# One kernel, a new order: a table of places for dynamic convolution, layer norm and feed-forward

## The chip, the cores and the metric

One NeuronCore of a Trainium2 chip runs the whole program. The metric is the device time of one execution in microseconds (us), the median of several. Five engines work side by side, each through its own list of instructions in its own fixed order: TensorE (PE; its weight loads are shown apart as PEld), VectorE (DVE), ScalarE (ACT), GpSimd (POOL) and SyncE (SP, which only issues transfers). They meet through semaphores. Transfers are carried by 16 DMA engines, whoever issues them.

## The reference

```python
# x (8, 4224, 192), weight_gen (8, 4224, 8 heads, 7 taps)
w = softmax(weight_gen, axis=-1)                 # over the 7 taps of each head
x_unf = the token and its 6 predecessors, zeros ahead of each sequence
out = np.einsum('bshk,bskhg->bshg', w, x_unf)    # 24 channels to a head
...
x = out                                          # (8, 4224, 192)
xn = (x - mean) / sqrt(var + 1e-06) * g_ln
return x + np.maximum(xn @ w_ch1, 0.0) @ w_ch2   # 192 -> 768 -> 192
```

`g_ln`, `w_ch1` and `w_ch2` come as 64-bit floats; everything else is 32-bit.

## The kernel before

The 33,792 tokens lie as 128 partitions by 264 columns: partition p holds 264 tokens that follow each other, and a column is 128 tokens, one on each partition. The work is cut three ways.

- **Chunks** (mostly 6 columns, 47 of them) are the unit of the convolution. SP loads x into a ring of 36 columns (`load`, L425). DVE makes the seven products of x and tap weights in four instructions, `c0` to `c3` (L507; three of them make two products at once, into two halves of a buffer `pr`, the fourth makes one, into `y`). POOL then issues two transfers that add one half of a `pr` to the other inside the DMA engines (`d0`, `d1`, L513; called adds below), and adds four halves to `y` with instructions of its own (`a0` to `a3`, L510). The first three chunks are small and are summed on PE (L532).
- **Parts** (mostly 12 columns, 25 of them) are the unit of the softmax weights and of the layer norm. ACT sums and squares each column (`sums` L571, `squares` L576), a few tiny instructions make the scale (`rstd` on ACT, `newton` on DVE, L603 to L608), ACT applies it (`xh`, L620) and makes a 16-bit copy (`hi`, L640), POOL makes the 16-bit remainder (`lo`, L642), and SP issues a transpose by DMA (`turn`, L646) into `xT`. The softmax of a load of 12 columns is `wload` (SP, L431), `max` and `sum` (DVE), `sub` and `less` (POOL, L451 and L458), `exp` and `log` (ACT).
- **Groups** (4 columns, 66 of them, numbered from 0; table entries are given by the group in which they begin) are the unit of the feed-forward part. A group has one `lo` and one `turn`. PE makes three `unit`s of 36 matmuls each from `xT` (L664), which go to two PSUM buffers `ph`; ACT writes relu as 16-bit numbers (`relu`, L679), and DVE their remainder (`hlo`, L681), which frees `ph`. The second product of a group runs one group later: `p0` and `p1`, 72 matmuls each (L715), between the next group's units. DVE adds the result to `y` (`f`, L767), and SP writes a chunk out (`u`, L775). For the last group, PE makes the second product in another form (L744).

At the start, SP also loads the two weight matrices; DVE, ACT, POOL and PE turn them into scaled 16-bit halves (names that begin with `w_`), and SP swaps halves of the first (`w_m`, L922), which has to land before the first `unit`.

**What sets the order.** The code records every operation with `op(engine, cost, (name, t), function, reads, writes)`, and the operation takes the next number from the table `PLACE[name]`. `Plan.order` sorts all operations by that number and issues them so; an engine's instructions stand in its list in this order and never overtake each other. The costs handed to `op` are not used for the order. The numbers run through all engines together. Which of a pool's buffers an operation gets also follows from the places:

```python
o.key, o.place = want, PLACE[want[0]][i]
...
out = sorted(self.ops, key=lambda o: o.place)
...
b.slot = min(range(len(tenant[b.pool])), key=lambda i: freed(tenant[b.pool][i]))
...
if o.kind in last:
    o.behind, last[o.kind] = last["turn" if o.kind == "add" else "add"], o
```

The last two lines keep adds and transposes apart: each add (`d0`, `d1`) waits until the last transpose placed ahead of it has landed, and each transpose until the last add placed ahead of it has. Nothing else orders transfers against each other.

The data the program needs between engines sets the other waits: a `turn` waits for `hi` and `lo`, the first `unit` of a group for its `turn`, and a third use of `ph` for an `hlo`.

## Time and profile before

| | |
|---|---|
| median of 3 runs | 884.35 us (879.41 to 884.49) |
| the profiled execution | 884.04 us |
| its span, first to last instruction | 882.2 us |
| PE busy | 822.3 us, 93% of the span |
| DVE, POOL, ACT busy | 740.9, 704.4, 690.1 us |
| mean granted clock of TensorE | 0.976 of full |

The profiled execution lies within 0.4 us of the median, and 1.84 us of it lie outside the span. A busy PE is one with a matmul in flight; a matmul that runs slowly is busy for longer, so the count of matmuls in a stretch tells more of progress than the busy time.

### The profile page before, as it was taken

What the parts mean: (1) busy time and instruction counts of PE and PEld (TensorE: products, weight loads), DVE (VectorE), ACT (ScalarE), POOL (GpSimd) and SP (SyncE); (2) the same over time, 40 slices, a digit from 0 to 9 for tenths busy, and PEclk for the clock granted to TensorE, in tenths of its full rate; (3) what the DMA queues carried; (4) which work ended last, traced back from release to release, by engine and by line L of the source; (5) the groups of instructions that cost most, each with busy time, mean ns of one, the idle gap of its engine ahead of it and who ended that gap; (6) DMA issues with size and microseconds to landing.
All of it is one profiled execution on the core that took longest, in us unless ns stands there. A gap on an engine that the chain in (4) does not pass through costs nothing.

```text
span 882.2 us, 37253 instructions
## 1 busy us (share of the span) xinstructions
PE 822.3 (93%) x16663; PEld 796.0 (90%) x16663; DVE 740.9 (84%) x670; ACT 690.1 (78%) x1796; POOL 704.4 (80%) x391
## 2 busy tenths in 40 slices
PE   5457899999999999999999999999999999989997
PEld 5237899999999899999999999999999999979997
DVE  7999999988999899899979889989998887844433
ACT  3689898998788769968897987978888887867421
POOL 4999999997989888799979889979998988735100
PEclk9759999999999999999999999999999999989999
DMA  8689687879996967777889798676878967553432
GB/s 222 150 194 197 142 182 187 182 153 214 214 199 134 215 140 156 168 150 154 171 170 202 146 218 181 165 168 161 199 126 172 213 134 136 110 83 51 108 74 82
DMA packets 135294, 141.66 MB, mean 161 GB/s; under 512 B 107238, under 2 KB 109166, under 8 KB 135134
## 3 DMA queue, kind: packets, MB, share of 16 engines
q1 hardware_dynamic: 122158, 88.94, 45.0%
q0 software_dynamic: 12672, 50.34, 29.3%
q8 instruction: 130, 2.13, 1.0%
q14 instruction: 30, 0.25, 0.1%
q10 hardware_dynamic: 304, 0.00, 0.0%
HBM read 36.43 MB, written 25.95 MB: 71 GB/s over the span
## 4 chain that ended last, share of the span: by engine, by line
PE 46%; POOL 30%; issue 8%; DMA 7%; DVE 5%; ACT 4%; SPq 0%; POOLq 0%; DVEq 0%; ACTq 0%
PE ph L664 23%; PE po L715 22%; POOL y L510 20%; POOL hl L642 4%; DMA xT<-hl 3%; POOL pr L513 3%; DVE pr L507 3%; DMA pr<-pr 3%; POOL e L451 1%; POOL e L458 1%; DVE hlo L681 1%; ACT junk L571 1%; ACT junk L576 1%; PE ph L744 1%; DMA x<-in_x_dram 1%
## 5 line engine op out<-in xcount | busy, mean ns | idle before, releaser
L510 POOL TENSOR_TENSOR y<-y,pr 128x1152 f32<-128x1152 f32 (+1 forms) x176 | 474.2, 2707 | 27.1 <-DVE y L507 13.1
L664 PE MATMUL ph<-xT,c_w 64*128 64x256 f16 x7128 | 419.4, 271 | 22.4 <-DMA xT<-hl 13.0
L664 PEld LDWEIGHTS <-c_w 64*128 64x128 f16 x7128 | 379.7, 95 | 38.8 <-DMA xT<-hl 15.0
L715 PE MATMUL po<-c_w2h,hh 64*128 64x192 f16 x3120 | 387.7, 243 | 6.0 <-DVE y L767 2.9
L715 PE MATMUL po<-c_w2h,hlo 64*128 64x192 f16 x3120 | 387.8, 243 | 1.5 <-issue 1.5
L715 PE MATMUL po<-c_w2l,hh 64*128 64x192 f16 x3120 | 387.7, 243 | 1.2 <-issue 1.2
L507 DVE TENSOR_TENSOR pr<-x,wn 128x2304 f32<-128x2304 f32 (+2 forms) x139 | 333.8, 2412 | 5.0 <-POOL y L510 2.9
L681 DVE SCALAR_TENSOR_TENSOR hlo<-ph,hh 128x1024 f16<-128x1024 f32 x198 | 239.4, 1219 | 97.7 <-ACT hh L679 96.6
L715 PEld LDWEIGHTS <-hh 64*128 64x128 f16 x6240 | 304.1, 94 | 9.9 <-issue 8.1
L679 ACT ACTIVATE hh<-ph 128x1024 f16<-128x1024 f32 x198 | 199.5, 1013 | 99.6 <-PE ph L664 92.0
L715 PEld LDWEIGHTS <-hlo 64*128 64x128 f16 x3120 | 172.4, 94 | 2.0 <-issue 1.8
L642 POOL TENSOR_TENSOR hl<-xh,hl 128x768 f16<-128x768 f32 x66 | 114.5, 1754 | 32.5 <-ACT hl L640 29.7
L620 ACT ACTIVATE xh<-y,s 128x192 f32<-128x192 f32 x264 | 125.5, 535 | 13.1 <-DVE s L608 5.5
L576 ACT ACTIVATE junk<-y,s 128x192 f32<-128x192 f32 x264 | 119.6, 453 | 7.7 <-PE po L715 1.0
L513 POOL DMA_DIRECT2D pr<-pr x88 | 85.0, 1065 | 44.2 <-DMA xT<-hl 17.0
L571 ACT ACTIVATE junk<-y 128x192 f32<-128x192 f32 x264 | 94.9, 360 | 19.9 <-POOL y L510 11.3
L767 DVE SCALAR_TENSOR_TENSOR y<-po,c_fs,y 128x768 f32<-128x768 f32 (+1 forms) x86 | 68.4, 813 | 5.0 <-PE po L715 4.6
L507 DVE TENSOR_TENSOR y<-x,wn 128x1152 f32<-128x1152 f32 (+2 forms) x47 | 59.6, 1267 | 1.7 <-ACT wn L470 1.7
L640 ACT ACTIVATE hl<-xh 128x768 f16<-128x768 f32 x66 | 55.0, 837 | 3.3 <-DMA xT<-hl 1.4
L571 ACT ACTIVATION_READ_ACCUMULATOR junk<-y 128x1 f32 x264 | 49.5, 187 | 0.0
L576 ACT ACTIVATION_READ_ACCUMULATOR junk<-y,s 128x1 f32 x264 | 49.4, 187 | 0.0
L451 POOL TENSOR_TENSOR e<-w,mx 128x672 f32<-128x672 f32 (+2 forms) x23 | 33.8, 1470 | 7.8 <-DVE mx L449 6.6
(76 smaller groups left out, 285.2 us busy)
## 6 DMA issues: line engine op xcount, KB each, us to landing
pr<-pr POOLq DMA_DIRECT2D x80, 576.0 KB, 6.8
x<-in_x_dram SPq DMA_DIRECT2D x40, 576.0 KB, 6.2
out_dram<-y SPq DMA_DIRECT2D x40, 576.0 KB, 6.1
w<-in_weight_gen_dram SPq DMA_DIRECT2D x21, 336.0 KB, 5.0
pr<-pr POOLq DMA_DIRECT2D x8, 384.0 KB, 4.5
x<-in_x_dram SPq DMA_DIRECT2D x5, 384.0 KB, 5.6
out_dram<-y SPq DMA_DIRECT2D x4, 384.0 KB, 3.5
x<-in_moe_w_ch_dram SPq DMA_DIRECT2D x1, 1152.0 KB, 13.3
```

The costliest lines, as they stand in the source:

```text
L507: E.tensor_tensor(out=ov, in0=xv, in1=wv, op=ALU.mult)
L510: Q.tensor_tensor(out=flat(0), in0=flat(0), in1=flat(k), op=ALU.add)
L513: return Q.dma_start(flat(to), flat(k), accum_op=ALU.add, max_dma_last_dim=CHUNK * D * 4)
L571: A.activation(junk, at(y)[:, j, :], AF.Identity, scale=-SQ / D, accum_out=at(s4)[:, 3, t : t + 1])
L576: A.activation(junk, at(y)[:, j, :], AF.Square, scale=SQ, bias=at(s4)[:, 3, t : t + 1], accum_out=at(s4)[:, 0, t : t + 1])
L620: A.activation(paired(xh, t), at(y)[:, i, :].rearrange("p (c q) -> p c q", q=P // 2), AF.Identity, bias=at(s4)[:, 3, g + t : g + t + 1], s ...
L642: lambda xh=xh, hl=hl: Q.tensor_tensor(out=halves(hl, True), in0=pairs(xh), in1=halves(hl, False), op=ALU.subtract),
L664: T_.matmul(ph[:, r, v * 2 * P : (v + 1) * 2 * P], W["w1"][rows, WB[r][c], w, f : f + P], xv[rows, a, c, :, :], start=(v == 0 and k == 0), ...
L679: lambda: A.activation(at(hh)[:, us, :], at(ph), AF.Relu), [ph], [(hh, u)])
L681: lambda: V.scalar_tensor_tensor(out=at(hlo)[:, us, :], in0=at(ph), scalar=0.0, in1=at(hh)[:, us, :], op0=ALU.max, op1=ALU.subtract),
L715: made.append(T_.matmul(at(po)[:, z, e * D : (e + 1) * D], token(b, 2 * z + e, j)[rows], W[w][rows, j, :], start=(ph == 0 and e == 0 and k ...
L767: V.scalar_tensor_tensor(out=ysl, in0=at(po)[:, zs[0] : zs[-1] + 1, : 2 * D], scalar=W["fs"][:, 0:1], in1=ysl, op0=ALU.mult, op1=ALU.add)
```

## The change

Only the numbers in `PLACE` are new: all 2,300-odd of them. The operations, their shapes, the buffers and their counts, the rule that keeps adds and transposes apart, and the engine of each operation are as before. Two lines of the table stand for the rest:

```diff
-    'w_load': (34, 36, 40, 85, 0, 1),
+    'w_load': (37, 17, 34, 1, 27, 67),
...
-    'halo': (184, 517, 711, 966, 1276, 1593, 2005),
+    'halo': (235, 545, 643, 1004, 1275, 1568, 2105),
```

Three places show what that does. In the rows, a name's number is a buffer's: `y_69` is one of nine `y`, `pr_77` one of five `pr`.

POOL, around the adds for the chunks that begin in groups 24 and 25 (columns 96 to 107): L513 is an add, L510 an addition to `y`, L642 a `lo`, L451 and L458 are softmax steps. Before:

```order
L458 TENSOR_TENSOR e_97<-e_97,sm_95 128x672
L510 TENSOR_TENSOR y_69<-y_69,pr_77 128x1152
L513 DMA pr_80<-pr_80 128x1152
L513 DMA pr_79<-pr_79 128x1152
L513 DMA pr_76<-pr_76 128x1152
L513 DMA pr_77<-pr_77 128x1152
L510 TENSOR_TENSOR y_74<-y_74,pr_78 128x1152
```

and now, the same four adds:

```order
L513 DMA pr_78<-pr_78 128x1152
L510 TENSOR_TENSOR y_67<-y_67,pr_80 128x1152
L642 TENSOR_TENSOR hl_84<-xh_82,hl_84 128x2x384
L642 TENSOR_TENSOR hl_83<-xh_81,hl_83 128x2x384
L510 TENSOR_TENSOR y_69<-y_69,pr_79 128x1152 x2
L513 DMA pr_80<-pr_80 128x1152
L510 TENSOR_TENSOR y_73<-y_73,pr_76 128x1152
L513 DMA pr_77<-pr_77 128x1152
L510 TENSOR_TENSOR y_73<-y_73,pr_76 128x1152
L510 TENSOR_TENSOR y_73<-y_73,pr_78 128x1152
L513 DMA pr_79<-pr_79 128x1152
```

Four adds that stood in a row have POOL's own work between them. In the whole list of POOL, three or more adds stand in a row at five places before, and at two now: one early, at the chunk that begins in group 4, and one at the very end.

SP, the transposes (L646) and outputs (L775) of the last groups. Before, from the transpose of group 57 to that of group 62; the fourth row is group 60's, and the sixth group 59's:

```order
L646 DMA_TRANSPOSE xT_85<-hl_84 128x12x128
L425 DMA x<-in_x_dram 128x1x768
L646 DMA_TRANSPOSE xT_86<-hl_83 128x12x128
L646 DMA_TRANSPOSE xT_87<-hl_83 128x12x128
L775 DMA out_dram<-y_70 16x8x1152
L646 DMA_TRANSPOSE xT_85<-hl_84 128x12x128
L646 DMA_TRANSPOSE xT_86<-hl_84 128x12x128
```

Now, from group 57's as well; the fourth row is group 59's, and the sixth group 60's:

```order
L646 DMA_TRANSPOSE xT_87<-hl_84 128x12x128
L646 DMA_TRANSPOSE xT_86<-hl_83 128x12x128
L775 DMA out_dram<-y_74 16x8x1152
L646 DMA_TRANSPOSE xT_85<-hl_84 128x12x128
L775 DMA out_dram<-y_68 16x8x1152
L646 DMA_TRANSPOSE xT_87<-hl_83 128x12x128
```

Group 59's transpose went behind group 60's and an output before, and is ahead of both now. On PE, one `unit` and two halves (`p0`, `p1`) stand in the table between its `lo` and its first `unit` before, and four `unit`s and four halves now.

DVE, the products of the last chunk (L507; `128x768` writes `y`), between `hlo` (L681) and `f` (L767). Before:

```order
L681 SCALAR_TENSOR_TENSOR hlo_90<-ph_105,hh_89 128x1024
L507 TENSOR_TENSOR pr_76<-x,wn_103 128x2x768
L681 SCALAR_TENSOR_TENSOR hlo_90<-ph_104,hh_89 128x1024
L767 SCALAR_TENSOR_TENSOR y_68<-po_106,c_fs,y_68 128x768
L681 SCALAR_TENSOR_TENSOR hlo_91<-ph_105,hh_88 128x1024
L507 TENSOR_TENSOR y_70<-x,wn_103 128x768
```

and now:

```order
L507 TENSOR_TENSOR y_74<-x,wn_102 128x768
L767 SCALAR_TENSOR_TENSOR y_68<-po_106,c_fs,y_68 128x768
L507 TENSOR_TENSOR pr_79<-x,wn_102 128x2x768
L681 SCALAR_TENSOR_TENSOR hlo_90<-ph_105,hh_88 128x1024
L681 SCALAR_TENSOR_TENSOR hlo_90<-ph_104,hh_88 128x1024
L507 TENSOR_TENSOR pr_78<-x,wn_102 128x2x768
L681 SCALAR_TENSOR_TENSOR hlo_90<-ph_105,hh_88 128x1024
L767 SCALAR_TENSOR_TENSOR y_75<-po_106,c_fs,y_75 128x768
L507 TENSOR_TENSOR pr_80<-x,wn_102 128x2x768
```

The chunk's `y` was the last of its four products, behind an `hlo` of group 59, and is the first of them now, ahead of all three `hlo` of group 58.

## Rows read from the trace of the kernel before

**Rows 1.** The page: busy time of each engine, share of the span, instructions.

```profile
PE 822.3 (93%) x16663; PEld 796.0 (90%) x16663; DVE 740.9 (84%) x670; ACT 690.1 (78%) x1796; POOL 704.4 (80%) x391
```

**Rows 2.** The span in stretches: busy us (instructions) by engine, granted clock, DMA share, GB/s.

```profile
100.00:150.00 50.00, 48.56 (x1023) 47.59 (x1019) 48.14 (x40) 44.43 (x124) 49.59 (x28) 1.00 0.77 176
...
300.00:350.00 50.00, 46.64 (x947) 45.96 (x944) 43.78 (x37) 39.85 (x100) 43.01 (x24) 0.97 0.78 168
350.00:400.00 50.00, 47.56 (x1002) 46.69 (x998) 43.61 (x36) 39.96 (x105) 42.28 (x22) 1.00 0.72 145
...
750.00:800.00 50.00, 45.95 (x936) 43.78 (x932) 29.28 (x29) 34.79 (x93) 30.13 (x21) 0.93 0.48 85
800.00:850.00 50.00, 50.00 (x1064) 47.01 (x1060) 21.89 (x30) 26.82 (x56) 8.82 (x6) 1.00 0.48 101
```

**Rows 3.** The chain that ended last, a steady stretch: start us, us, what.

```profile
134.97 2.97 PE po L715 x72
137.94 3.93 PE ph L664 x72
...
146.80 2.97 PE po L715 x72
```

**Rows 4.** What PE waited for: us in total, times, longest us.

```profile
PE ph L664 <- DMA xT<-hl: 13.0, 5, 6.9
PE ph L664 <- DVE hlo L681: 7.0, 6, 2.3
PE po L715 <- issue: 5.4, 6, 1.9
...
PE ph L664 <- issue: 2.2, 4, 0.7
```

**Rows 5.** PE in order of time, the first unit: start us, us, work [idle before <-releaser].

```profile
59.39 6.43 PE L664 MATMUL ph<-xT,c_w 64*128 64x256 f16 x72 [6.94 <-DMA xT<-hl]
```

**Rows 6.** The chain's last pieces on PE, and PE at 785.98 in order of time.

```profile
871.55 6.06 PE ph L744 x72
785.98 6.65 PE L664 MATMUL ph<-xT,c_w 64*128 64x256 f16 x72 [4.05 <-DMA xT<-hl]
```

**Rows 7.** POOL in order of time, three of four adds (the fourth went at 295.79).

```profile
289.68 2.66 POOL L513 DMA_DIRECT2D pr<-pr  x3 [0.52 <-DMA xT<-hl]
```

**Rows 8.** Stretches from these adds on, columns as in rows 2.

```profile
289.00:302.00 13.00, 13.00 (x276) 12.89 (x273) 11.80 (x14) 10.49 (x25) 9.03 (x8) 1.00 1.03 208
302.00:306.00 4.00, 2.06 (x47) 1.89 (x45) 3.90 (x4) 3.79 (x6) 4.00 (x3) 1.00 0.90 180
306.00:320.00 14.00, 13.66 (x256) 13.31 (x252) 10.54 (x8) 8.46 (x24) 12.09 (x6) 0.88 0.89 208
```

**Rows 9.** PE in order of time, in the second of these stretches.

```profile
305.82 0.26 PE L715 MATMUL po<-c_w2h,hh 64*128 64x192 f16 x2 [1.94 <-issue]
```

**Rows 10.** SP in order of time: transpose of group 60, an output, transpose of group 59.

```profile
774.65 1.38 SPq L646 DMA_TRANSPOSE xT<-hl  x1
776.14 0.99 SPq L775 DMA_DIRECT2D out_dram<-y  x1
777.24 4.29 SPq L646 DMA_TRANSPOSE xT<-hl  x1
```

**Rows 11.** POOL in order of time, from there to the `lo` of group 61.

```profile
786.47 0.88 POOL L513 DMA_DIRECT2D pr<-pr  x1 [8.48 <-DMA xT<-hl]
793.28 5.58 POOL L510 TENSOR_TENSOR y<-y,pr 128x768 f32<-128x768 f32 x3 [5.93 <-DVE y L507]
798.82 1.65 POOL L642 TENSOR_TENSOR hl<-xh,hl 128x768 f16<-128x768 f32 x1
```

**Rows 12.** The view of the tile `xT`: transposes from issue to landing, all 66.

```profile
DMA to landing us min/median/max: 3.2/4.2/9.5
```

**Rows 13.** The page: POOL's additions to `y`: count, busy us, mean ns, idle before.

```profile
L510 POOL TENSOR_TENSOR y<-y,pr 128x1152 f32<-128x1152 f32 (+1 forms) x176 | 474.2, 2707 | 27.1 <-DVE y L507 13.1
```

**Rows 14.** The page: the DMA queue of PE's instructions: packets, MB, share of 16 engines.

```profile
q8 instruction: 130, 2.13, 1.0%
```

## The prediction

> **What bounds the kernel now.** I began with the busy times: PE leads with 93% [rows 1], and of the others only DVE comes to 84%. The end of the chain agrees: PE works without a pause until 877.61 (871.55 + 6.06) [rows 6], 4.6 us before the span ends. So the time is what PE has to do, plus what it waits, plus the time to its first unit.

> What it has to do is read from a steady stretch of the chain. From one `p0` at 134.97 to the next at 146.80 lie three units and two halves: 11.83 us a group [rows 3]. The program holds 65 such groups, three units ahead of them (1.5 times the 3.93 us of two units, 5.9 us) and the last output (6.06 us): 5.9 + 65 x 11.83 + 6.1 = 781 us. The first unit starts at 59.39 [rows 5], PE ends at 877.61: 818 us for 781 us of work. **37 us are lost after the first unit**, and 59 us go before it. Nothing on any other engine shortens the 781.

> Where the 37 us lie is best read from the count of matmuls in stretches of 50 us. At full rate a stretch has 252 x 50 / 11.83 = 1065; the one at 800 shows 1064 [rows 2]. A missing matmul is then 47 ns. The 15 stretches from 100 to 850 us hold 15,500 instead of 15,960: 21.6 us lost, and the rest of the 37 lies in the opening up to 100 us. Three stretches hold most of the 21.6: 300 to 400 us (117 + 62 missing, 8.4 us) and 750 to 800 us (128 missing, 6.0 us) [rows 2]. A few records can be missing from a trace, so I trust these to about 1 us.

> What PE waited for is the next view. It names transposes (13.0 us, 6.94 of them ahead of the first unit [rows 4, 5]), `hlo` (7.0 us), and "issue", which means that the profile shows nothing it waited for: 5.4 + 2.2 = 7.6 us in ten waits [rows 4].

> **The middle: adds in a row.** The largest of the ten comes at 305.82, 1.94 us in the midst of the 72 matmuls of a half, where no data can be missing [rows 9]. Just before, POOL issued three adds in a row and soon a fourth [rows 7]; the DMA engines were full for 13 us (share 1.03) while PE ran, and PE got half of the next 4 us [rows 8]. PE's own instructions come by DMA too: 130 packets, 2.13 MB [rows 14], about one in 6 us. I read the waits for "issue" as packets of instructions that came late behind transfers. [...] All ten and this: 7.6 + 1.7 = 9.3 us.

> The change takes the adds apart: POOL's list has five places with three or more adds in a row before, and two now, none of them between the opening and the last groups. It takes nothing away: the same 88 adds move the same bytes. So of 9.3 us the gain lies between 0 (the crowd only forms elsewhere) and 9.3. Since all five crowds of before go, one of them ahead of the costliest stop, I take nearer to the upper end: **-7.5 us**.

> [...]

> **The end: group 59.** At 785.98 PE starts a unit after 4.05 us of waiting for a transpose, and two units then take 6.65 us [rows 6] instead of 3.93 [rows 3], as after the first wait, where they took 6.43 [rows 5]: 4.05 + 2.72 = 6.8 us. That transpose was issued at 777.24, behind that of group 60, which nobody needed yet, and an output [rows 10]; it was 8.7 us on its way, where the median is 4.2 [rows 12]. The new list has group 59's ahead of both, and its `lo` 4 units and 4 halves ahead of its first unit (4 x 1.97 + 4 x 2.97 = 19.8 us) instead of 7.9 us. That stall should go.

> What is late next is group 61. Before, POOL came to its `lo` at 798.82 after two waits: 8.48 us at an add kept behind the late transpose, and 5.93 us for the `y` of the last chunk from DVE [rows 11]. Both have their causes moved: the transpose is earlier, and that `y` now is the first of its chunk's products on DVE instead of the last. So the bounds are 0 and -6.8; near the upper one, with a little left for group 61: **-6.5 us**.

> **The opening.** SP still has the four swaps of weights ahead of the first transpose, so the first unit stays near 59.4. Summing what stands ahead in each list by the durations of this trace: DVE has 2.0 us less ahead of the first `hlo`; POOL has the same ahead of the `lo` of groups 2 and 3, and one addition more, 2.7 us [rows 13], ahead of those of groups 4 and 6. POOL was busy there almost without a pause (49.59 of 50 us [rows 2]), so more work ahead is delay. Between -2.0 and +2.7 I take **+1 us**.

> **New short leads.** In three groups of the middle (21, 24 and 48) the new table leaves one unit and one half, 4.94 us, between `lo` and first unit; before, no group after the opening had less than 7.9. A `lo` of 1.65 us [rows 11] and a transpose of 3.2 at best [rows 12] fill that with nothing to spare. The price of one that fails is that of group 59, 6.8 us; bounds 0 and 20 us. But transposes that are placed, as issues, 4.94 us or less ahead of their unit (11 after group 6 before, and 12 now) cost little before: besides the first unit and group 59, PE waited for transposes for 13.0 - 6.94 - 4.05 = 2.0 us in all [rows 4 to 6]. I take **+2 us**.

> The other waits for DVE are reshuffled with no sign that I can read: 0. **Sum:** 884.04 - 7.5 - 6.5 + 1 + 2 = **873.0 us**. The profiled execution lies 0.3 us under the median, so this stands for the median as it is.

> **The rivals.**

> *The waits for "issue" stay (a).* They move with the transfers, or are no late packets at all. [...] In rows: only the end is gained, 884 - 6.5 + 3 = 880.5.

> *The feeders are the bound (b).* POOL, DVE and ACT are busy for 80, 84 and 78% [rows 1], and a `y` buffer comes free only when PE's result is out. If PE stops less, it catches up with the transposes and waits for them instead. For it: every stop of PE that an earlier wait would have covered is repaid by the next one. Against it: 15,500 of 15,960 matmuls is 97% of full rate, with the feeders at work in 13 of the 15 stretches. Time 884.

> *The short leads fail (c), the slower side.* At groups 21, 24 and 48 the transposes land 2 us or more after PE is ready, each stops PE and then lowers its clock: 3 x 6.8 = 20.4 us, with the crowds as before, 2.7 us in the opening, and only the end gained: 884 + 20.4 + 2.7 - 6.5 = 900.5. It decides from about two of the three on. For it: 4.94 us against 4.85 in the best case. Against: the 2.0 us that all other short issues cost before.

> *Nearly all goes (d).* All 9.3 and 6.8 us and some of the waits for `hlo`: 884 - 16 - 4 = 864.

> **How the numbers follow.** My forecast 0.52 (866 to 882, two thirds of it under 875.5), (a) 0.15, (b) 0.09, (c) 0.12, (d) 0.12. Runs of the kernel before differ by 0.6% among themselves, so about 1% (8.8 us) is what a measurement can tell from no change. Faster by more: 0.52 x 0.65 + 0.12 = 0.46. Slower by more: 0.12. Within: 0.42. The range leaves out the lower half of (d) and most of (c): 863 to 891.

> **What would show it.** If right, the stretches between 300 and 400 us come to over 1,040 matmuls each, and PE's waits for "issue" to under 3 us; the unit of group 59 starts without a wait, and the clock in 750 to 800 is 1.00; the period stays 11.83 us; the first unit starts between 57 and 62 us. If wait lines for transposes in the middle add up to over 8 us, (c) is at work; if "issue" stays at 7 us, (a). What would make the forecast wrong is a stall that no list shows: a crowd of transfers of several queues together at a place where SP waits longer than the table thought.

## The result, and the profile after

The changed kernel takes 872.4 us (median of 4 runs, 869.5 to 874.1), the kernel before 883.2 us (median of 4, 879.4 to 884.5): a ratio of 0.988, with a 95% interval of 0.984 to 0.993. The profiled execution took 874.1 us with a span of 872.2, beside 884.0 and 882.2 before.

The page, busy time of each engine, share of the span and instructions, as in [rows 1]:

```profile
PE 818.9 (94%) x16663; PEld 799.2 (92%) x16663; DVE 740.0 (85%) x670; ACT 689.1 (79%) x1796; POOL 704.7 (81%) x391
```

The same work, 10 us sooner. Where, the stretches of [rows 2] tell (busy us and instructions of PE, PEld, DVE, ACT and POOL, then granted clock, DMA share, GB/s):

```profile
100.00:150.00 50.00, 47.21 (x966) 44.31 (x962) 48.78 (x39) 44.34 (x122) 49.61 (x27) 0.97 0.80 174
300.00:350.00 50.00, 48.07 (x1023) 46.99 (x1019) 46.49 (x37) 37.86 (x90) 44.16 (x25) 1.00 0.90 187
350.00:400.00 50.00, 49.99 (x1057) 49.55 (x1053) 45.67 (x39) 44.53 (x128) 43.52 (x23) 1.00 0.80 157
750.00:800.00 50.00, 50.00 (x1069) 50.00 (x1067) 31.07 (x32) 38.45 (x100) 32.25 (x21) 1.00 0.57 106
```

The three stretches that were poor have gained 76, 55 and 133 matmuls; 750 to 800 now runs at full rate and full clock. The stretch from 100 to 150, at the end of the opening, has lost 57: not everything went the right way. What PE waited for (us in total, times, longest), to be held against [rows 4]:

```profile
PE ph L664 <- DMA xT<-hl: 15.2, 4, 8.9
...
PE ph L664 <- DVE hlo L681: 6.2, 12, 1.0
...
PE po L715 <- issue: 0.9, 2, 0.5
```

The waits for "issue" fell from 7.6 us to 0.9. The waits for transposes rose, all in the opening but for one, which PE in order of time shows (the third row is the unit of group 59, [rows 6]):

```profile
62.41 6.51 PE L664 MATMUL ph<-xT,c_w 64*128 64x256 f16 x72 [8.86 <-DMA xT<-hl]
...
324.23 4.10 PE L664 MATMUL ph<-xT,c_w 64*128 64x256 f16 x72 [1.93 <-DMA xT<-hl]
...
777.97 4.11 PE L664 MATMUL ph<-xT,c_w 64*128 64x256 f16 x72
```

The first unit is 3.0 us later than before [rows 5]. Group 59 starts without a wait and runs at full rate. The chain that ended last, at a unit of group 6 and at its end, as in [rows 3, 6]:

```profile
142.24 3.93 PE ph L664 x72
...
849.61 3.93 PE ph L664 x72
...
861.45 6.06 PE ph L744 x72
```

The steady period is 861.45 - 849.61 = 11.84 us, as it was. With that the 10 us can be split. The unit of group 6 starts at 142.24, 4.3 us later than the 137.94 of [rows 3]. From there to group 59 lie 53 groups, 627.5 us at full rate. Before, it took 785.98 - 137.94 = 648.0 us, 4.05 of them the wait at group 59, so 16.5 were lost on the way; now it takes 777.97 - 142.24 = 635.7, and 8.2 are lost. Opening +4.3, middle -8.3, group 59 with its slow matmuls -6.8, small things later +0.6: together -10.2 us, and the two executions differ by 9.9.

### The profile page after: what moved, and what is told of

Its sections match the earlier page's. It is cut to its first block, busy times and chain, and to the rows that moved or that the text cites. A ratio compares the mean times of both kernels' runs of the same rounds, so it can differ in the third digit from the quotient of the medians.

```text
span 872.2 us, 37235 instructions
## 1 busy us (share of the span) xinstructions
PE 818.9 (94%) x16663; PEld 799.2 (92%) x16663; DVE 740.0 (85%) x670; ACT 689.1 (79%) x1796; POOL 704.7 (81%) x391
## 3 DMA queue, kind: packets, MB, share of 16 engines
q8 instruction: 130, 2.13, 1.0%
## 4 chain that ended last, share of the span: by engine, by line
PE 50%; POOL 12%; ACT 7%; issue 6%; DVE 5%; DMA 5%; POOLq 0%; ACTq 0%; SPq 0%; DVEq 0%
PE ph L664 25%; PE po L715 25%; POOL y L510 8%; DMA xT<-hl 2%; DMA pr<-pr 2%; DVE pr L507 2%; ACT hh L679 2%; ACT junk L571 2%; DVE hlo L681 2%; POOL hl L642 2%; POOL pr L513 1%; ACT xh L620 1%; ACT junk L576 1%; PE ph L744 1%; POOL e L458 1%
## 5 line engine op out<-in xcount | busy, mean ns | idle before, releaser
L510 POOL TENSOR_TENSOR y<-y,pr 128x1152 f32<-128x1152 f32 (+1 forms) x176 | 478.5, 2736 | 25.9 <-DVE y L507 12.7
L664 PE MATMUL ph<-xT,c_w 64*128 64x256 f16 x7128 | 418.5, 271 | 21.6 <-DMA xT<-hl 15.2
L664 PEld LDWEIGHTS <-c_w 64*128 64x128 f16 x7128 | 384.5, 95 | 32.3 <-DMA xT<-hl 17.3
L507 DVE TENSOR_TENSOR pr<-x,wn 128x2304 f32<-128x2304 f32 (+2 forms) x139 | 334.1, 2413 | 6.3 <-issue 3.3
L715 PEld LDWEIGHTS <-hh 64*128 64x128 f16 x6240 | 317.5, 94 | 2.4 <-ACTq L725 1.8
L681 DVE SCALAR_TENSOR_TENSOR hlo<-ph,hh 128x1024 f16<-128x1024 f32 x198 | 239.3, 1220 | 90.3 <-ACT hh L679 89.5
L715 PEld LDWEIGHTS <-hlo 64*128 64x128 f16 x3120 | 187.9, 94 | 1.6 <-issue 1.6
L642 POOL TENSOR_TENSOR hl<-xh,hl 128x768 f16<-128x768 f32 x66 | 115.5, 1782 | 43.3 <-ACT hl L640 34.2
L513 POOL DMA_DIRECT2D pr<-pr x88 | 86.2, 1052 | 30.9 <-DVE pr L507 17.1
L767 DVE SCALAR_TENSOR_TENSOR y<-po,c_fs,y 128x768 f32<-128x768 f32 (+1 forms) x86 | 68.7, 815 | 6.9 <-PE po L715 6.7
L507 DVE TENSOR_TENSOR y<-x,wn 128x1152 f32<-128x1152 f32 (+2 forms) x47 | 59.6, 1268 | 0.9 <-ACT wn L470 0.9
L458 POOL TENSOR_TENSOR e<-e,sm 128x672 f32<-128x672 f32 (+2 forms) x23 | 34.8, 1515 | 9.0 <-ACT sm L456 9.0
```

Source lines behind the costliest of these rows:

```text
L507: E.tensor_tensor(out=ov, in0=xv, in1=wv, op=ALU.mult)
L510: Q.tensor_tensor(out=flat(0), in0=flat(0), in1=flat(k), op=ALU.add)
L513: return Q.dma_start(flat(to), flat(k), accum_op=ALU.add, max_dma_last_dim=CHUNK * D * 4)
L642: lambda xh=xh, hl=hl: Q.tensor_tensor(out=halves(hl, True), in0=pairs(xh), in1=halves(hl, False), op=ALU.subtract),
L664: T_.matmul(ph[:, r, v * 2 * P : (v + 1) * 2 * P], W["w1"][rows, WB[r][c], w, f : f + P], xv[rows, a, c, :, :], start=(v == 0 and k == 0), ...
L681: lambda: V.scalar_tensor_tensor(out=at(hlo)[:, us, :], in0=at(ph), scalar=0.0, in1=at(hh)[:, us, :], op0=ALU.max, op1=ALU.subtract),
```

## The experiments

Times are medians. Each group of runs had its own runs of the kernel before beside it (880.1 to 881.3 us), and the ratios are against those.

### Taking the stages apart

First, the old opening with everything else new.

```diff
-all operations in the order of the changed kernel
+the first 450 in the order of the kernel before, the rest as in the changed kernel
```

> The first 450 operations stand in the order of the kernel before (through the first units of group 6), all others in that of the changed kernel. Theory (stages add up): in the changed kernel the first unit came 3.0 us later (62.41 against 59.39) and that of group 6 came 4.3 us later; with the old opening back these 4.3 us come back and nothing else changes: 872.4 - 4.3 = 868.1, first unit at 59 to 60, group 6 at 137 to 139. Rival (the feeders bind, what PE gains early it waits away later): 872.4, with new waits for transposes of about 4 us between groups 7 and 40.

Measured: 867.45 us, ratio 0.985 (0.982 to 0.988). PE's first unit, and what PE waited for in its units (no row for "issue" is left in either product):

```profile
59.06 6.56 PE L664 MATMUL ph<-xT,c_w 64*128 64x256 f16 x72 [7.05 <-DMA xT<-hl]
```

```profile
PE ph L664 <- DMA xT<-hl: 9.0, 4, 7.0
...
PE ph L664 <- DVE hlo L681: 8.6, 10, 2.1
```

The time came back and stayed back. (The expected 868.1 is 4.3 us under the changed kernel; 867.45 was measured.) This order beats both kernels, and none of the study is faster.

Second, the old opening and middle with the new end.

```diff
-all operations in the order of the kernel before
+the first 2,080 as before, the last 288 in the order of the changed kernel
```

> The first 2,080 operations stand in the order of the kernel before (through its middle, to the units of group 56), the last 288 in that of the changed kernel. Theory (stages add up): only the stop at group 59 goes, -6.8 us, and group 62 gives back 0.5: 883.2 - 6.3 = 876.9, the two units of group 59 in about 4 us without a wait, the waits for issue still 5 to 9 us. Rival (the middle alone made the gain, the stop at 59 is paid later): 882 to 883, a new wait at groups 60 to 62 of 4 us or more.

Measured: 874.25 us, ratio 0.994 (0.992 to 0.996). Group 59's wait is gone. Its profiled execution was the longest of eleven (880.0 us), and "issue" had 8.1 + 3.4 = 11.5 us in it, so the old middle still has its price.

The changed kernel itself was run again for a base:

> The changed kernel once more, beside the three below on one chip, so that they can be held against it: 0.985 to 0.993 of the kernel before, first unit at 62 to 63, waits for issue under 2 us in all.

Measured: 872.18 us, ratio 0.991 (0.988 to 0.994), "issue" 2.0 us. By medians the three stages are now: end 874.25 - 880.41 = -6.2, middle 867.45 - 874.25 = -6.8, opening 872.18 - 867.45 = +4.7 (across two groups of runs). That these add up to the whole means nothing, since each splice is the base of the next. What counts is that each stage, measured by the time of the whole run, has about the size that the trace gave it (-6.8, -8.3 and +4.3). So the rival that what is won early is waited away later has fallen.

### Group 59 alone

```diff
-POOL: lo 60, lo 59     SP: turn 60, u 57, turn 59
+POOL: lo 59, lo 60     SP: turn 59, u 57, turn 60
```

> The kernel before; only the remainders and transposes of groups 59 and 60 have changed places, so that the transpose of 59 stands ahead of an output and of that of 60. Theory (the transpose stood in the wrong row): it is issued 2.6 us earlier and without company, lands in about 4 instead of 8.7 us, so all of the 4.05 us wait and the 2.7 us of slow matmuls after it go: -6 us, 877. Rival (its remainder comes too late on POOL whatever SP does, and group 61 is next late): -2.3 us or less, 881 to 883, with a wait left at group 59 or a new one at 61.

Measured: 873.36 us, ratio 0.992 (0.990 to 0.994): -7.0 us for two swapped pairs. SP in order of time, the rows of [rows 10] with group 59's transpose first now, and PE at that group's unit:

```profile
771.07 2.08 SPq L646 DMA_TRANSPOSE xT<-hl  x1
773.26 0.56 SPq L775 DMA_DIRECT2D out_dram<-y  x1
```

```profile
778.17 4.11 PE L664 MATMUL ph<-xT,c_w 64*128 64x256 f16 x72
```

Issued at 771.07 in place of 777.24, it was there in time. PE had no wait for a transpose behind group 59 either, so group 61 was not next late. The swap alone brings as much as the whole new end did (-6.2), so the gain of the end comes from this place.

### What makes the waits for "issue"

Spreading the adds in the old order:

```diff
 POOL, at one of five places (13 adds moved in all)
-d0:24 d1:24 d1:25.5 d0:25.5 a0:25.5 a2:24 sub:33 a3:24
+d0:24 a0:25.5 d1:24 a2:24 d1:25.5 sub:33 a3:24 d0:25.5
```

> The kernel before; at the five places where three or four adds stood in a row (chunks of groups 12, 24, 45, 48 and 57) 13 adds stand one or two POOL instructions later, so that no two of them follow each other; nothing else moves. Theory (adds in a row hold up PE's instruction packets): the waits for issue fall from 7.6 us to under 3 and the slow matmuls after them go too: -5 to -8 us, 875 to 878. Rival (the waits come from the whole flow of transfers, or are no matter of transfers): they stay at 5 to 9 us, perhaps elsewhere, 881 to 884.

Measured: 884.9 us, ratio 1.006 (1.003 to 1.008): slower. What PE waited for, and PE at the new and the old stop:

```profile
PE ph L664 <- DMA xT<-hl: 16.0, 6, 6.9
...
PE ph L664 <- DVE hlo L681: 9.8, 8, 2.2
...
PE ph L664 <- issue: 2.1, 3, 1.0
PE po L715 <- issue: 2.1, 2, 1.6
```

```profile
176.15 5.77 PE L664 MATMUL ph<-xT,c_w 64*128 64x256 f16 x72 [3.00 <-DMA xT<-hl]
...
787.86 5.73 PE L664 MATMUL ph<-xT,c_w 64*128 64x256 f16 x72 [3.94 <-DMA xT<-hl]
```

"Issue" fell to 4.2 us, not under 3, and the time went the wrong way: an add that stands later goes out later, and a transpose waits for the last add ahead of it. At the first of the five places the three adds went out by 151.91 before, the last of them at 159.67 now, and the next two transposes at 165.40 and 168.32 in place of 161.69 and 166.12. The unit at 176.15 waited 3.00 us, and the two units from there took 5.77 us in place of 3.93. Both theories missed the time.

Next, 68 of the 88 adds left out (the outputs then lack two of the seven products):

```diff
         for i, k in enumerate((1, 3)):
+            if 48 <= t0 < 250:
+                plan.count[f"d{i}"] += 1
+                continue
             op("Pool", 610, (f"d{i}", t0), ...
```

> The kernel before without the transfers that add one half of a product buffer to the other for the chunks that begin in groups 12 to 62 (68 of 88 adds are left out, so their outputs lack two of the seven products); all else in its old order. Theory (PE's instruction packets come late behind crowds of transfers of any queue, and adds are the larger part of each crowd): the waits for issue fall from 7.6 us to under 2.5. Rival 1 (SyncE's loads and outputs in a row suffice): 4 to 7 us stay, at 207 and 320 above all. Rival 2 (no matter of transfers): 6 to 9 us, all in their old places. The time falls by 5 us or more in either case, since transposes no longer wait for adds, and decides nothing.

Measured: 870.98 us, ratio 0.989 (0.985 to 0.992). The rows for "issue" (lines are three higher in this kernel):

```profile
PE ph L667 <- issue: 1.0, 2, 0.7
PE po L718 <- issue: 0.9, 1, 0.9
```

1.9 us: without these adds the other transfers, in their old order, hardly stop PE. Are rows of adds enough to bring the waits back? Rows put into the changed kernel:

```diff
 POOL, at one of eight places
-d0:27 a0:28.5 less:33 d1:27 sub:36 d0:28.5 a2:27 d1:28.5
+a0:28.5 less:33 sub:36 d0:27 d1:27 d0:28.5 d1:28.5 a2:27
```

> The changed kernel; at eight places of its middle the adds of two chunks, which had POOL's own work between them, stand in a row of three or four at the place of the last of them (chunks of groups 24, 27, 31.5, 39, 42, 45, 54 and 57); SyncE's list is untouched. Theory (a row of adds alone holds up PE's packets): the waits for issue rise from 1 to 2 us to 5 to 10, time +4 to +10. Rival 1 (a row of adds does it only with a crowd of loads and outputs beside it, which this list no longer has): issue stays under 3 us, time within 2 us. Rival 2 (the price of adds is their lateness, since the sums of a chunk and so its transpose come later): waits for transposes and hlo rise by 3 us or more, with issue under 3.

Measured: 886.7 us, ratio 1.006 (1.004 to 1.009), 14.5 us over the changed kernel. What PE waited for, and one row of what DVE waited for:

```profile
PE ph L664 <- DVE hlo L681: 13.7, 18, 2.5
...
PE ph L664 <- issue: 0.7, 1, 0.7
...
PE po L715 <- issue: 0.4, 1, 0.4
```

```profile
DVE pr L507 <- POOL y L510: 8.0, 5, 3.4
```

Eight rows of adds, and 1.1 us of "issue". The time went elsewhere: the adds that had to wait for their row hold their `pr` buffers for longer, DVE waits for a free one (8.0 us; 1.7 when the changed kernel was run again), and its `hlo` come late (13.7 us of waiting on PE; 4.4). **My theory that a row of adds is enough to stop PE fell here.**

Crowds of loads and outputs instead:

```diff
 SP, at one of 15 places
-load:34.5 turn:21 u:17 turn:23 load:30 u:20
+turn:21 turn:23 load:30 u:20 load:34.5 u:17
```

> The changed kernel; at 15 places of its middle one to four of SyncE's loads and outputs stand later, right behind others, so that three or four go out in a row while adds are in flight; loads only where the products need them 35 us later or more; adds, POOL, DVE, ACT and PE keep their order. Theory (late packets behind crowds of any transfers): the waits for issue come back, from 0.9 us to 5 to 15, and the time rises by 4 to 15 us. Rival 1 (only adds in a row do it): issue stays under 2 us, time within 2 us. Rival 2 (a crowd holds up transposes, not packets): waits for transposes rise by 5 us or more with issue under 2.

Measured: 895.64 us, ratio 1.017 (1.014 to 1.021). One row of what DVE waited for, and two of PE:

```profile
DVE y L507 <- DMA out_dram<-y: 18.8, 4, 8.1
```

```profile
PE ph L664 <- DVE hlo L681: 22.3, 16, 7.8
...
PE po L715 <- issue: 3.4, 5, 1.3
```

Slower by more than any theory said, and hardly by packets. An output that goes out late keeps its `y`, and the next product on DVE stands until it has gone (18.8 us); the `hlo` behind it are what PE waits for (22.3 us). The next run leaves the outputs alone:

```diff
-load:34.5 turn:21 u:17 turn:23 load:30 u:20
+turn:21 u:17 turn:23 load:30 u:20 load:34.5
```

> The changed kernel; as in the run with crowds, but only ten loads stand later, right behind other loads or outputs, and every output is back at its place. Theory (the slow run with crowds was slow because late outputs held the y buffers that DVE's products need): DVE's wait for outputs falls from 18.8 us to under 2, the time comes back to within 3 us of the changed kernel, issue 1 to 4 us. Rival (loads in a row are what costs): +6 us or more over the changed kernel, with waits for issue or transposes to match.

Measured: 874.33 us, ratio 0.992 (0.989 to 0.995). DVE's wait for outputs is gone, the time is back to 2.2 us over the changed kernel (across two groups of runs), and "issue" has one row:

```profile
PE po L715 <- issue: 3.1, 4, 1.6
```

Last, SP's whole middle exchanged between the kernels, once each way:

```diff
-SP: 76 loads and outputs between groups 7 and 57 as in this kernel
+SP: the same 76 where the other kernel has them, counted by PE's progress
```

> The kernel before; only SyncE's 76 loads and outputs between groups 7 and 57 stand where they stand in the changed kernel, counted by PE's progress (a few of DVE's maxima moved with their loads); adds, transposes and all of POOL's, ACT's and PE's orders are the old ones, the rows of adds with them. Theory (packets come late where loads and outputs crowd in among adds, so SyncE's order is what matters): the waits for issue fall from 7.6 us to under 3, time -3 to -7 against the kernel before, the stop at group 59 stays. Rival (the rows of adds are what matters after all): issue 5 to 9 us, time within 2 us.

> The reverse: the changed kernel; SyncE's 76 loads and outputs between groups 7 and 57 stand where they stood in the kernel before, counted by PE's progress; adds spread as in the changed kernel. Theory (SyncE's order): issue rises from 1 to 2 us to 4 to 8, time +3 to +7 against the changed kernel. Rival (rows of adds): issue stays under 3, time within 2 us.

Measured: 905.9 us, ratio 1.026 (1.022 to 1.031), and 908.23 us, ratio 1.032 (1.028 to 1.036). Both are far slower than either parent. What DVE waited for, in the first and in the second:

```profile
DVE mx L449 <- DMA w<-in_weight_gen_dram: 17.0, 5, 7.9
```

```profile
DVE y L507 <- DMA out_dram<-y: 10.8, 3, 5.6
DVE mx L449 <- DMA w<-in_weight_gen_dram: 9.8, 2, 7.5
```

DVE's wait for this load came to 3.3 us in the kernel before and 2.3 in the changed one, and neither had a row for outputs. SP's transposes waited for adds for up to 24.4 us at a time in the first run and 26.9 in the second, and what stands behind such a transpose in SP's list waits along (with the adds apart, a load behind one went at 172.45 in place of 168.76). That the late loads and outputs stood there is my reading; no row shows it. What PE waited for as "issue", in the first (in the longest of its six executions, 915 us) and in the second:

```profile
PE po L715 <- issue: 9.6, 4, 4.1
...
PE ph L664 <- issue: 2.3, 1, 2.3
```

```profile
PE po L715 <- issue: 1.6, 2, 1.0
...
PE ph L664 <- issue: 0.7, 1, 0.7
```

That is 11.9 and 2.3 us. By that alone the adds' places would matter and SP's would not. But DVE's stalls here (17.0 us; 10.8 and 9.8) are ones that neither parent has at that size, so these two runs count for less than the others.

All profiles together. PE's instructions come in packets of 128 matmuls each (shown in the last section). The last column counts packets in the trace: of the 99 of the middle (matmuls 1,400 to 14,100), those that began to move more than 3 us after PE had taken up the packet before.

| order of the middle | "issue", us | late packets |
|---|---|---|
| old | 7.6; 11.5 (new end); 6.4 (59 swapped) | 23; 26; 23 |
| old, adds apart | 4.2 | 14 |
| old, adds left out | 1.9 | 11 |
| old, SP's loads and outputs as changed | 11.9 | 16 |
| new | 0.9; 2.0; 1.5 and 0 (two mended openings) | 4; 2; 3 and 3 |
| new, adds in eight rows | 1.1 | 11 |
| new, loads and outputs crowded | 3.4 | 10 |
| new, loads crowded | 3.1 | 9 |
| new, SP's loads and outputs as before | 2.3 | 13 |

Executions of one middle differ by 2 us or more in "issue", but by 3 at most in late packets, so the last column separates the runs better. From about 3 late packets in the new middle, rows of adds lead to 11, loads in rows to 9, and SP's old list to 13. From about 24 in the old middle, setting the adds apart leads to 14, leaving them out to 11, and SP's new list to 16. So the places of the adds and SP's list each delay packets, neither alone makes up the whole difference, and most of these late packets do not stop PE (the kernel before has 23 and ten stops).

### The opening

ScalarE in order of time, in the changed kernel (a small load, then the first exponential):

```profile
7.32 0.38 ACTq L800 DMA_DIRECT2D c_g<-in_moe_g_ln_dram  x1
7.80 0.39 ACT L452 ACTIVATE w<-e 128x224 f32<-128x224 f32 x1 [5.18 <-DMA x<-in_x_dram]
```

The first exponential waited 5.18 us behind the issue of a load of 0.5 KB at most, which itself, by the profile, had to wait for a load of `x`. In the kernel before:

```profile
3.36 1.82 ACTq L800 DMA_DIRECT2D c_g<-in_moe_g_ln_dram  x2
5.23 0.39 ACT L452 ACTIVATE w<-e 128x224 f32<-128x224 f32 x1 [2.61 <-DMA w<-in_weight_gen_dram]
```

There, two such loads also stood ahead of the exponential, but they were issued at 3.36, and it ran at 5.23. Why the one load had to wait and the two did not, no run shows. So:

```diff
 ACT
-w_load exp:0 log:0 expw:0 expw:0.5 keep:0.5 exp:1 keep:0 w_load log:1 ... expw:3 w_load
+exp:0 log:0 expw:0 expw:0.5 keep:0.5 exp:1 keep:0 log:1 ... expw:3 w_load w_load w_load
```

> The changed kernel; only ScalarE's first two loads of the layer norm's scale (0.2 to 0.5 KB each) now stand right ahead of its third, behind the first three exponentials. Theory (ScalarE's list stands still behind the first small load, whose issue had to wait for a load of x to land at 7.24, so its first exponential ran at 7.80 instead of 5.23 and the whole opening slipped by 3 us): first exponential at 5.2 to 5.5, first unit at 59 to 60.5, time 2 to 3.5 us under that of the changed kernel. Rival (SyncE's new order of the first loads sets the opening): the first exponential is early but products still wait for x, first unit stays at 62 to 63, time within 1 us.

Measured: 868.66 us, ratio 0.987 (0.984 to 0.990), 3.5 us under the changed kernel in the same group of runs. The same exponential, and PE's first unit:

```profile
4.43 0.39 ACT L452 ACTIVATE w<-e 128x224 f32<-128x224 f32 x1 [1.81 <-POOL e L451]
```

```profile
59.55 6.33 PE L664 MATMUL ph<-xT,c_w 64*128 64x256 f16 x72 [8.88 <-DMA xT<-hl]
```

Two small loads, moved on one list, are worth 3 us at PE 55 us later. That is most of what the new opening lost.

## Why the prediction came true, and where it did not

The forecast was 873.0 us, the result is 872.4. The total is right for reasons that are half right, and that it fits so closely is in part luck: the forecast is 11.0 us under the profiled execution before, the medians here differ by 10.8 us, and by 8.1 us when the changed kernel was run again (872.18 beside 880.31).

- **PE is the bound** at 11.83 us a group: right, 11.84 in the changed kernel at full rate.
- **The end, -6.5 us**: right in size (-6.8 in the trace, -6.2 and -7.0 by two experiments) and in cause, shown by the swap alone. "What is late next is group 61" did not come true: its `lo` ran at 792.18 (798.82 before [rows 11]), and PE did not wait.
- **The middle, -7.5 us for adds in a row**: the size is about right, the cause is half right. The waits for "issue" fell from 7.6 to 0.9 us, and the middle brought 6.8 to 8.3 us with the short leads in it. The step that failed is "all five crowds of before go, one of them ahead of the costliest stop": I counted adds on POOL's list alone and put SP's new order of loads and outputs at nothing. Setting the same adds apart in the old order took away only 3.4 of the 7.6 us (4.2 were left) and 9 of 23 late packets, and lengthened the run; rows of adds in the new order brought late packets back (11), but hardly a stop (1.1 us). SP's list has its own part: alone, though with stalls of its own, it took the late packets from about 3 to 13 in the new order. How the two together hold a packet back is not settled. The 9.3 us that the -7.5 was taken from hold 1.7 us that no run shows as such. What the trace before shows after the stop at 305.82 is a granted clock of 0.50 from 306.60 to 309.90 and 42 matmuls there, where the full rate has 70: 28 missing, 1.3 us.
- **The rival that the waits are no late packets** falls: each of the ten stands where one packet ends and the next begins, and ends 1.3 to 1.6 us after a late packet (last section). In the kernel before, a packet began to move only about when PE took up the one before it (1.2 us later by median).
- **The opening, +1 us**: wrong, +4.3 in the trace and +4.7 by the experiments, beyond the bound of +2.7. I summed what stands ahead on DVE and POOL and left out ScalarE's list, which now begins with a transfer whose issue had to wait. The diff of `w_load` in this text shows that very move (the fourth number, 85 before and 1 now).
- **Short leads, +2 us**: right in sum. Of groups 21, 24 and 48 only the first stopped PE, for 1.93 us, and none did in the second profile of the same kernel (its three waits for transposes all lie in the opening). But the price of a failed one was not 6.8 us: the two units after it took 4.10, so it cost 2.1.
- **The signs to look for**: "issue" under 3 us, group 59 and its clock, the period and the waits for transposes in the middle (1.93 us) came as said; 1,057 matmuls in 350 to 400, but 1,023 and not over 1,040 in 300 to 350, where group 21's stop lies; the first unit missed its window (62.41, not 57 to 62).

By the trace, the opening's miss of 3.3 us was nearly covered by a middle that gained 2.8 us more than the -5.5 I had for it; by the experiments the miss is 3.7 us and the middle's surplus 1.3. These errors had nothing to do with each other; that they offset is luck.

## What to carry to other kernels

When a whole order is exchanged, splice the two orders at a place where both work on the same thing and run the halves: here each stage came out of the splices at about its size in the trace, and the splice of the old opening with the new rest beat both. Read every engine's list at the start, above all for transfers issued by an engine that computes: such an issue waits in order, and what stands behind it waits along (5.18 us here). A transfer moved later was paid for by the buffer that it kept (18.8 us of DVE's waiting for a `y`, 8.0 us for a `pr`); two swapped pairs at the right place were worth as much as the whole new middle (-7.0 and -6.8 us).

## What the runs showed of the hardware that was not expected

**PE's waits for "issue" keep their place in PE's list, whatever the time.** In the kernel before and in the run with its end exchanged, PE in order of time:

```profile
482.90 3.34 PE L664 MATMUL ph<-xT,c_w 64*128 64x256 f16 x58 [0.67 <-issue]
```

```profile
484.26 3.34 PE L664 MATMUL ph<-xT,c_w 64*128 64x256 f16 x58 [0.79 <-issue]
```

Both stop with 58 of 72 matmuls left; so does the run with group 59 swapped, at 479.44, and the one with adds apart, at 482.63. The page of the kernel before gives 16,663 matmuls and as many weight loads to 130 packets: 256 instructions, or 128 matmuls, to a packet. Counted through PE's list, the ten stops of the kernel before have 1,885, 2,909, 4,957, 5,213, 5,725, 6,237, 8,541, 9,437, 13,149 and 13,277 matmuls ahead of them. Each of these numbers leaves 93 when divided by 128, and all 65 such stops in the profiles of this study leave 93 or 94. So these stops stand at the seams between packets.

**A short stop need not cost more than itself.** In the changed kernel, the 6 us after a wait of 2.62 us at 104.54 and the 4 us after the 1.93 us at 324.23, columns as above:

```profile
104.50:110.50 6.00, 5.96 (x82) 4.68 (x84) 6.00 (x5) 4.39 (x13) 5.92 (x4) 0.72 0.83 237
324.20:328.40 4.20, 4.17 (x78) 3.74 (x80) 4.20 (x5) 3.13 (x11) 4.20 (x3) 1.00 1.09 184
```

The clock fell after the first (0.72 of full over the stretch, 0.50 from 104.95 to 108.30; two units took 5.77 us) and not after the second (1.00, 4.10 us). Length alone does not tell which: the stop at 305.82 in the kernel before was as short as the second, 1.94 us [rows 9], and the clock fell after it (0.88 over 14 us [rows 8]). I had priced each failed short lead as if its matmuls would run slowly afterwards.
